# A cubic in depressed form for VectorE's share of the softmax exponentials

## The chip, the cores and the metric

The kernel runs on one core of one Trainium2 chip. The metric is the device time of one execution in microseconds (us), and a kernel's time is the median of its runs. A profile is one execution, taken by the hardware profiler. The engines are written as in the profile: PE is TensorE (matmuls), ACT is ScalarE, DVE is VectorE, POOL is GpSimd, SP is SyncE.

## The reference

Two layers follow one another, each an attention block and a token mixer. Cut to what matters:

```python
def _A_ref(x, wqkv, wo):                    # x: 1 x 2048 x 640, 32 heads of 20
    qkv = ...                               # x @ wqkv, split into q, k, v by heads
    scores = einsum("bhqd,bhkd->bhqk", q, k) * (Dh ** -0.5)
    p = softmax(scores, axis=-1)
    o = einsum("bhqk,bhkd->bhqd", p, v)
    return ... @ wo
def _B_ref(x, w1, b1, w2, b2):              # mixes tokens: 2048 -> 1536 -> 2048
    h = layernorm(x)
    u = gelu(einsum("bsd,sf->bdf", h, w1) + b1)
    return ...                              # einsum("bdf,fs->bds", u, w2) + b2, transposed
x = x + _A_ref(layernorm(x), A_wqkv, A_wo)
x = x + _B_ref(layernorm(x), B_w1, B_b1, B_w2, B_b2)
...                                         # the same two lines once more
```

A layer needs 32 x 2048 x 2048 exponentials of scores. They are by far the largest elementwise work.

## The kernel before

**Units and chunks.** A layer's attention is cut into 512 units: one block of 512 queries, one group of four heads, one tile of 128 keys. Each unit has four chunks, one for a head: 128 keys by 512 queries of scores. `s_matmul` (L703) makes the scores of a chunk in PSUM, already scaled so that the integer part is the power of two wanted times 65536. `emit_PV` (L1334) multiplies the exponentials of a unit with the values (`Vaug`) and adds to `acc`.

**Who takes the exponentials.** `emit_exp` (L773) gives two or three chunks at a time to ScalarE, from a tile `S` to a tile `P`. Some chunks go to VectorE instead. `ve_admit` takes one chunk at a time while the bank `Dt` is free, VectorE's backlog is at most 7 us and at most two pairs are waiting; two chunks make a pair `p`.

**VectorE's exponential.** It builds the bits of a bf16 number as an integer, in these steps of a pair:

- `first` (L563), once for each chunk: adds 127 * 65536 to the score in `Dt`, clips at zero and writes an int32 to the tile `ew`. Its upper 16 bits are the exponent (`whole`), its lower 16 the fraction (`frac`). Both are read with a step of two 16-bit words.
- `shift` (L661): a shifted fraction in f16, to the tile `ey`. Mostly done by GpSimd, chunk by chunk (`ve_shift`), on VectorE only where GpSimd has not done it (`shifted`).
- `squared` (L593): `ey` times itself, 1024 columns, in place.
- `mantissa` (L597): (ey + constant) * frac, one three-operand instruction over 1024 columns, to the tile `et` as an int16. There is one `et` buffer.
- `expo` (L614 and L616): 128 * whole + et, to `Pd`, read as bf16 by the product. GpSimd may already have written 128 * whole for a chunk (`ve_base`, L644). If it did so for both, VectorE adds `et` in one instruction (L614, 1024 columns). If for none, one three-operand instruction does it all (L616, 1024 columns). If for one, each half has its own instruction (L614 and L616, 512 columns).

**What sets the order.** The order on VectorE, ScalarE and GpSimd is written out when the program is built, by a planner that replays the engines with constants for the cost of every step. `Proc` is a chain of steps; `Proc.step` moves the engine's clock to the step's end less 0.083 (`DVE_OVER`) and lets the chain's next step start 0.034 (`DVE_NEXT`) after that end. `pump` picks, of the chains that can start, the one of the lowest rank; evacuations for TensorE have ranks 0 to 2, a pair's chain has 4, and only the oldest pair may go on. The costs of a pair's steps stand in one place:

```python
cost = VE_ADD[min(2, len(ve_based.get(p, [])) + 2 - k)]    # VE_ADD = (1.22, 1.03, 0.69)
steps += [(0.69, squared, 0.0, True), (1.22, mantissa, 0.0, True), (cost, expo, 0.0, True)]
```

The last `True` marks steps beside which GpSimd gets no work. GpSimd's `shift` and base steps are put beside VectorE's other steps of at least 0.45 us, and each waits for the VectorE instruction ahead of that host (`after_vector`).

TensorE's queue follows the same plan; where nothing useful is due it gets products with zeros (`zero_wave`, L762). VectorE takes exponentials in the first layer from early on, in the second one only after the mixer of the layer before has been worked off beside the first units.

Of the kernel before, what the change touches and what calls it, by code (L numbers as in the profile page):

```python
# [15 lines left out]
I16 = mybir.dt.int16  # L16
U16 = mybir.dt.uint16
F16 = mybir.dt.float16
ACT = mybir.ActivationFunctionType
ALU = mybir.AluOpType  # L20
# [43 lines left out]
POOL_BASE_HOST = 0.45  # L64
VEP_BUFS = 4
VE_SPARE = 6
VE_ADD = (1.22, 1.03, 0.69)
POOL_DMA = 0.9

HOLD = 3  # L70
# [1 line left out]
LOG2E = 1.4426950408889634  # L72
LN2 = 0.6931471805599453
FIX = 65536.0
MANT = (0.07706715865, 0.22764486, 0.69511682)
MANT_S = -0.5 * MANT[1] / MANT[0]
MANT_C = MANT[2] / MANT[0] - MANT_S ** 2
MANT_K = (MANT[0] * 128.0 / FIX) ** 0.5


@with_exitstack
def kernel(
# [12 lines left out]
    nc = tc.nc  # L95
# [11 lines left out]
    def after_vector(inst):  # L107
        earlier = next(i for i in reversed(nc.cur_bb.bb.instructions) if i.engine == nc.vector.engine)
        tc.add_manual_dep(inst.ins, earlier.name,
                          mybir.DependencyInfo(mybir.DependencyClass.Sync, mybir.DependencyReason.DATA), reason="port")  # L110
# [113 lines left out]
    def attention(st, x_in_ap, x_mid, uacc_l, feed, feed_stack):  # L224
# [14 lines left out]
        late, ve = {}, {}  # L239
# [284 lines left out]
        def ve_admit(t):  # L524
# [41 lines left out]
            def firsted(end):  # L566
                pieces.append((p, slot, w, end))
                bases.append((p, slot, w, end))
                if slot == 1:
                    ve_enqueue(p, 2, end + DVE_NEXT)  # L570
# [5 lines left out]
        def ve_enqueue(p, k, ready):  # L576
            w = ve_w.pop(p)
            wh = w[:, 0:k, :].rearrange("p a b -> p (a b)").bitcast(I16).rearrange("p (c two) -> p c two", two=2)
            frac = wh[:, :, 0].bitcast(U16)
            whole = wh[:, :, 1]  # L580
            box = {}

            def shifted(end):
                todo = [x for x in range(k) if x not in ve_shifted[p]]
                c0, c1 = 512 * todo[0], 512 * (todo[-1] + 1)
                for x in list(pieces):
                    if x[0] == p:
                        pieces.remove(x)
                shift(nc.vector, ve_y_of(p)[:, c0:c1], frac[:, c0:c1])

            def squared(end):
                y = ve_y_of(p)[:, 0:512 * k]
                nc.vector.tensor_tensor(out=y, in0=y, in1=y, op=ALU.mult)  # L593

            def mantissa(end):
                box["t"] = ve["vet"].tile([128, 1024], I16, name="et")
                nc.vector.scalar_tensor_tensor(out=box["t"][:, 0:512 * k], in0=ve_y.pop(p)[:, 0:512 * k],  # L597
                                               scalar=MANT_C * MANT_K ** 2, in1=frac, op0=ALU.add, op1=ALU.mult)

            def expo(end):  # L600
                Pd = ve_result(p)
                ve_P[p] = Pd
                ve_ready[p] = end + DVE_TO_PE
                ve_procs.popleft()
                for x in [x for x in bases if x[0] == p]:
                    bases.remove(x)
                based = ve_based.pop(p, [])
                parts = [range(k)] if len(based) in (0, k) else [[x] for x in range(k)]
                for part in parts:
                    lo, hi = 512 * part[0], 512 * (part[-1] + 1)  # L610
                    bits = Pd[:, 0:k, :].rearrange("p a b -> p (a b)").bitcast(I16)[:, lo:hi]
                    t = box["t"][:, lo:hi]
                    if part[0] in based:
                        nc.vector.tensor_tensor(out=bits, in0=bits, in1=t, op=ALU.add)  # L614
                    else:
                        nc.vector.scalar_tensor_tensor(out=bits, in0=whole[:, lo:hi], scalar=128.0, in1=t,  # L616
                                                       op0=ALU.mult, op1=ALU.add)
            steps = [(0.15 + 0.27 * (k - len(ve_shifted[p])), shifted, 0.0, True)] if len(ve_shifted[p]) < k else []
            cost = VE_ADD[min(2, len(ve_based.get(p, [])) + 2 - k)]
            steps += [(0.69, squared, 0.0, True), (1.22, mantissa, 0.0, True), (cost, expo, 0.0, True)]  # L620
            proc = Proc(4, steps, ready, allow=lambda me: ve_procs[0] is me and
                        (len(me.steps) > 1 or p in ve_results or p - VEP_BUFS not in ve_users))
            proc.pair, proc.ready = p, max([ready] + ve_shifted_at.get(p, []))
            ve_procs.append(proc)
            dvm["procs"].append(proc)
# [3 lines left out]
        def ve_result(p):  # L629
            if p not in ve_results:  # L630
                ve_results[p] = ve["vep"].tile([128, 2, 512], BF16, name="Pd")
            return ve_results[p]

        def ve_base(at):
            for x in bases:
                p, slot, w, end = x
                if end + POOL_NEXT > at + POOL_LATE or port["t"] > at + POOL_LATE:
                    return
                if p not in ve_results and (p - VEP_BUFS in ve_users or p - 1 not in ve_results and p > 0):
                    return  # L640
                bases.remove(x)
                bits = ve_result(p)[:, slot, :].bitcast(I16)
                whole = w[:, slot, :].bitcast(I16).rearrange("p (c two) -> p c two", two=2)[:, :, 1]
                after_vector(nc.gpsimd.tensor_scalar(out=bits, in0=whole, scalar1=128.0, scalar2=0.0, op0=ALU.mult, op1=ALU.add))  # L644
                port["pool"] = port["t"] = max(at + POOL_NEXT, end + POOL_NEXT, port["t"]) + POOL_EY
                ve_based.setdefault(p, []).append(slot)
                for proc in ve_procs:
                    if proc.pair == p:
                        cost, fn, wait, lock = proc.steps.pop()
                        proc.steps.append((VE_ADD[len(ve_based[p])], fn, wait, lock))  # L650
                return

        ve_y, ve_shifted, ve_shifted_at = {}, {}, {}

        def ve_y_of(p):
            if p not in ve_y:
                ve_y[p] = ve["vey"].tile([128, 1024], F16, name="ey")
            return ve_y[p]

        def shift(engine, out_ap, in_ap):  # L660
            return engine.tensor_scalar(out=out_ap, in0=in_ap, scalar1=MANT_K / FIX, scalar2=-MANT_K * MANT_S,  # L661
                                        op0=ALU.mult, op1=ALU.add)

        def ve_shift(at, self_cost):
            if (not pieces or pieces[0][3] + POOL_NEXT > at + POOL_LATE or port["t"] > at + POOL_LATE or
                    pieces[0][0] - 2 in ve_y):
                if self_cost >= POOL_BASE_HOST:
                    ve_base(at)
                return
            p, slot, w, end = pieces.popleft()  # L670
            half = w[:, slot, :].bitcast(I16).rearrange("p (c two) -> p c two", two=2)[:, :, 0].bitcast(U16)
            inst = shift(nc.gpsimd, ve_y_of(p)[:, 512 * slot:512 * (slot + 1)], half)
            after_vector(inst)
            done = max(at + POOL_NEXT, end + POOL_NEXT, port["t"]) + POOL_EY
            port["pool"] = port["t"] = done
            ve_shifted[p].append(slot)
            ve_shifted_at.setdefault(p, []).append(done + POOL_TO_DVE)
            for proc in ve_procs:
                if proc.pair == p:
                    cost, fn, wait, lock = proc.steps.popleft()  # L680
                    if cost > 0.5:
                        proc.steps.appendleft((cost - 0.27, fn, wait, lock))
                    proc.ready = max(proc.ready, done + POOL_TO_DVE)
# [749 lines left out]
        t = 0  # L1433
# [423 lines left out]
    with ExitStack() as a_stack:  # L1857
        st0 = open_a_scope(0, a_stack)
        open_p_scope(st0, a_stack)
        feed_stack = ExitStack()  # L1860
        feed = TokenFeed(feed_stack)
        attention(st0, A_x[0], xd[0], uacc[0], feed, feed_stack)
    with ExitStack() as a_stack:
        st1 = open_a_scope(1, a_stack)
        open_p_scope(st1, a_stack)
        feed_stack = ExitStack()
        feed = MixFeed(feed_stack, xd[0], xd[1], st0.ua)
        attention(st1, xd[1], xd[0], uacc[1], feed, feed_stack)
# [32 lines left out]
```

## Time and profile before

| | |
|---|---|
| median of 3 runs | 1750.6 us (1750.33 to 1750.99) |
| the profiled execution | 1751.01 us, span 1748.9 us |
| granted TensorE clock | 1.00 |
| busy: PE, ACT, DVE, POOL | 1666.2, 1666.9, 1538.9, 599.6 us |
| L773, exponentials on ACT | 1429 instructions, 1617.1 us |
| L563 to L616, exponentials on DVE | 262 pairs of chunks |
| L762, products with zeros on PE | 324.6 us |

Busy times are those of the profiled execution; the span runs from its first instruction to its last, and the rest of its time lies around that. A row of the profile's groups reads: line, engine, operation, output<-inputs by the program's names, shapes, number, then the busy time in us and the mean of one instruction in ns, then the idle time ahead of them and what ended most of it. VectorE's instructions overlap at their ends, so their durations add up to more than the engine's time.

### The profile page before, as it was taken

The page shows a single profiled execution, that of the slowest core. Times are in us where ns is not written, and L with a number is a line of the kernel's source. Part 1 is how long each engine was busy: PE and PEld are TensorE (multiplying, and loading weights), DVE is VectorE, ACT ScalarE, POOL GpSimd, SP SyncE. Part 2 cuts the span into 40 slices and gives each one's busy share as a digit, 9 for nine tenths or more (in the row PEclk, how much of TensorE's full clock was granted, in tenths as well). Part 3 has the DMA queues.
Part 4 walks back from the last instruction along what each step waited for, and adds up shares of the span by engine and source line. Part 5 has one row for each costly group of instructions (what it writes and reads, how often), then busy time and mean ns, then how long its engine had stood idle before and what let it go on. Part 6 is the DMA issues. An engine that isn't in the chain of part 4 may idle for free.

```text
span 1748.9 us, 43173 instructions
## 1 busy us (share of the span) xinstructions
PE 1666.2 (95%) x17767; PEld 664.3 (38%) x17848; DVE 1538.9 (88%) x2502; ACT 1666.9 (95%) x1498; POOL 599.6 (34%) x948
## 2 busy tenths in 40 slices
PE   8999999999999999999999999999999999999999
PEld 3333333333333343444444433333333333444445
DVE  7789999999999999998544479999999999999973
ACT  9999999999999999999779999999999999999970
POOL 2243443353544343332000023444434443534410
PEclk9999999999999999999999999999999999999999
DMA  4020000000122010133322200001001220211345
GB/s 117 9 23 10 1 2 2 24 24 2 35 66 83 25 42 7 40 90 104 116 78 75 65 11 1 1 2 39 24 2 54 63 85 20 92 29 29 81 121 176
DMA packets 103062, 81.85 MB, mean 47 GB/s; under 512 B 51025, under 2 KB 87505, under 8 KB 102865
## 3 DMA queue, kind: packets, MB, share of 16 engines
q1 hardware_dynamic: 97328, 71.22, 13.8%
q0 software_dynamic: 5536, 7.88, 1.4%
q8 instruction: 139, 2.28, 0.6%
q14 instruction: 59, 0.48, 0.1%
HBM read 55.48 MB, written 23.59 MB: 45 GB/s over the span
## 4 chain that ended last, share of the span: by engine, by line
ACT 51%; PE 25%; issue 22%; DVE 1%; DMA 0%; SPq 0%; another core or an unknown queue 0%; POOL 0%; ACTq 0%; DVEq 0%
ACT P L773 51%; PE S L703 7%; PE acc L1334 4%; PE ya L1784 2%; PE misc L1075 2%; PE acc L762 2%; PE misc L1184 2%; PE um L1771 1%; PE Dt L1184 1%; PE ya L1793 1%; PE yb L1784 1%; PE misc L1124 0%; PE Dt L1703 0%; PE misc L1208 0%; PE misc L1703 0%
## 5 line engine op out<-in xcount | busy, mean ns | idle before, releaser
L773 ACT ACTIVATE P<-S 128x1536 bf16<-128x1536 f32 (+1 forms) x1429 | 1617.1, 1373 | 13.5 <-PE S L703 13.1
L703 PE MATMUL S<-QTq,KT 32*128 32x512 bf16 (+1 forms) x4476 | 578.2, 336 | 65.0 <-ACT P L773 48.3
L661 POOL TENSOR_SCALAR ey<-ew 128x512 f16<-128x512 uint16 x512 | 317.8, 621 | 681.7 <-DVE et L597 295.5
L703 PEld LDWEIGHTS <-KT 32*128 32x128 bf16 x5152 | 232.3, 91 | 524.8 <-issue 497.4
L563 DVE TENSOR_SCALAR ew<-Dt 128x512 int32<-128x512 f32 x524 | 357.0, 681 | 21.2 <-PE Dt L703 14.7
L1334 PE MATMUL acc<-P,Vaug 128*32 128x512 bf16 (+1 forms) x4444 | 362.2, 343 | 0.1
L597 DVE SCALAR_TENSOR_TENSOR et<-ey,ew 128x1024 int16<-128x1024 f16 x262 | 326.0, 1244 | 2.8
L762 PE MATMUL acc<-zr,zw 128*32 128x512 bf16 x4184 | 324.6, 382 | 1.2 <-POOL zr L155 1.2
L644 POOL TENSOR_SCALAR Pd<-ew 128x512 int16<-128x512 int16 x333 | 206.8, 626 | 168.4 <-DVE et L597 44.7
L703 PE MATMUL Dt<-QTq,KT 32*128 32x512 bf16 (+1 forms) x676 | 201.4, 334 | 0.0
L593 DVE TENSOR_TENSOR ey<-ey 128x1024 f16<-128x1024 f16 x262 | 189.5, 723 | 1.4 <-POOL ey L661 0.3
L1334 PEld LDWEIGHTS <-Vaug 128*32 128x32 bf16 x5120 | 102.5, 94 | 169.5 <-issue 157.5
L762 PEld LDWEIGHTS <-zw 128*32 128x32 bf16 x4408 | 111.1, 96 | 96.7 <-issue 50.9
L614 DVE TENSOR_TENSOR Pd<-Pd,et 128x1024 int16<-128x1024 int16 (+1 forms) x197 | 129.8, 659 | 5.5 <-POOL Pd L644 3.3
L616 DVE SCALAR_TENSOR_TENSOR Pd<-ew,et 128x1024 int16<-128x1024 int16 (+1 forms) x126 | 123.5, 980 | 0.6
L903 POOL TENSOR_TENSOR rstd<-veps,mhalf 128x1 f32<-128x1 f32 x60 | 49.8, 830 | 212.9 <-DVE veps L901 194.1
L1334 PE MATMUL acc<-Pd,Vaug 128*32 128x512 bf16 (+1 forms) x676 | 103.0, 337 | 0.3 <-DVE Pd L614 0.2
L1184 PE MATMUL misc<-hh,wq_pad 128*128 128x512 bf16 x255 | 75.8, 383 | 2.8 <-issue 1.6
L1184 PE MATMUL misc<-hh,wk_pad 128*128 128x512 bf16 x240 | 73.3, 383 | 2.6 <-issue 1.9
L1075 PEld LDWEIGHTS <-w1st 128*128 128x128 bf16 x672 | 52.5, 97 | 57.6 <-issue 45.4
L1124 PE MATMUL misc<-wo_pad,attnT 128*128 128x320 bf16 x384 | 72.1, 302 | 0.0
L1075 PE MATMUL misc<-x1last,w1st 128*128 128x320 bf16 x384 | 71.8, 302 | 0.0
(146 smaller groups left out, 1187.5 us busy)
## 6 DMA issues: line engine op xcount, KB each, us to landing
w2s<-in_B_w_dram SPq DMA_DIRECT2D x16, 768.0 KB
uacc<-ustg POOLq DMA_DIRECT2D x24, 320.0 KB, 2.7
x1in<-xd SPq DMA_DIRECT2D x24, 320.0 KB
w1st<-in_B_w_dram SPq DMA_DIRECT2D x24, 256.0 KB
xd<-x2s SPq DMA_DIRECT2D x16, 320.0 KB
xin<-xd SPq DMA_DIRECT2D x16, 320.0 KB
w1st<-in_B_w_dram SPq DMA_DIRECT2D x21, 192.0 KB
xd<-x1s SPq DMA_DIRECT2D x12, 320.0 KB
```

The source lines that it names most:

```text
L563: nc.vector.tensor_scalar(out=w[:, slot, :], in0=Dt[:, :], scalar1=127.0 * FIX, scalar2=0.0, op0=ALU.add, op1=ALU.max)
L593: nc.vector.tensor_tensor(out=y, in0=y, in1=y, op=ALU.mult)
L597: nc.vector.scalar_tensor_tensor(out=box["t"][:, 0:512 * k], in0=ve_y.pop(p)[:, 0:512 * k], scalar=MANT_C * MANT_K ** 2, in1=frac, op0=ALU ...
L614: nc.vector.tensor_tensor(out=bits, in0=bits, in1=t, op=ALU.add)
L644: after_vector(nc.gpsimd.tensor_scalar(out=bits, in0=whole, scalar1=128.0, scalar2=0.0, op0=ALU.mult, op1=ALU.add))
L661: return engine.tensor_scalar(out=out_ap, in0=in_ap, scalar1=MANT_K / FIX, scalar2=-MANT_K * MANT_S, op0=ALU.mult, op1=ALU.add)
L703: pe(nc.tensor.matmul(out_ap[:, c0:c0 + w], lhsT=KT[32 * j:32 * j + 32, g, kt * 128:(kt + 1) * 128], rhs=get_QT(st, qb)[32 * j:32 * j + 32 ...
L762: pe(nc.tensor.matmul(bank[32 * j:32 * j + 32, 0:w], lhsT=zw[:], rhs=zr[:, :, 0:64].to_broadcast([128, w // 64, 64]), start=start, stop=st ...
L773: nc.scalar.activation(out=P[:, 0:ncs, :].rearrange("p a b -> p (a b)"), in_=St[:, 0:ncs, :].rearrange("p a b -> p (a b)"), func=ACT.Exp, ...
L1075: pe(nc.tensor.matmul(t[:, 0:w], lhsT=w1_of[(p, ft)][:, sti, :], rhs=rows_in[sti][:, c0:c1], start=(sti == 0), stop=(sti == n_in - 1)))
L1184: pe(nc.tensor.matmul(t[:, :], lhsT=wpad[:, dt_, g, :], rhs=hT[:, dt_, tb * 512:(tb + 1) * 512], start=(dt_ == 0), stop=(dt_ == NDT - 1)))
L1334: pe(nc.tensor.matmul(acc[32 * j:32 * j + 32, a0:a0 + w], lhsT=Vaug[:, (kt * H + hh_) * VW:(kt * H + hh_) * VW + 32], rhs=P[:, slot, c0:c0 ...
```

## The change

The polynomial for the fraction f, a cubic through 0 at 0 and about 128 at 1, is written without its quadratic term: with y proportional to f + 0.916 it is y * (y * y + A) - 66. The steps become:

- `squared` writes y * y to `et` (now an f16 tile) and leaves y in `ey`.
- `slope`, new: adds the constant A to `et` in place, one input, 1024 columns of f16.
- `mantissa`: `et` times `ey`, two inputs, f16 in, int16 out, in place in `et`.
- `expo`: the -66 goes into the base, 128 * whole - 66. Halves without a base from GpSimd get it from VectorE in one `set_base` instruction; then one addition of 1024 columns follows in all three cases.

The shift has other constants. The planner's costs become 0.69, 0.43, 0.69 and (1.3, 1.03, 0.69).

```diff
-VE_ADD = (1.22, 1.03, 0.69)
+VE_ADD = (1.3, 1.03, 0.69)
+VE_SLOPE = 0.43
...
-MANT = (0.07706715865, 0.22764486, 0.69511682)
-MANT_S = -0.5 * MANT[1] / MANT[0]
-MANT_C = MANT[2] / MANT[0] - MANT_S ** 2
-MANT_K = (MANT[0] * 128.0 / FIX) ** 0.5
+MANT_0 = -66.0
+MANT = (0.08063961, 0.49462884, -0.91643084)
+MANT_K = (128.0 * MANT[0]) ** (1.0 / 3.0)
+MANT_A = 128.0 * MANT[1] / MANT_K
...
             def squared(end):
                 y = ve_y_of(p)[:, 0:512 * k]
-                nc.vector.tensor_tensor(out=y, in0=y, in1=y, op=ALU.mult)
+                box["q"] = ve["vet"].tile([128, 1024], F16, name="et")
+                nc.vector.tensor_tensor(out=box["q"][:, 0:512 * k], in0=y, in1=y, op=ALU.mult)
+
+            def slope(end):
+                q = box["q"][:, 0:512 * k]
+                nc.vector.tensor_scalar(out=q, in0=q, scalar1=MANT_A, scalar2=None, op0=ALU.add)
 
             def mantissa(end):
-                box["t"] = ve["vet"].tile([128, 1024], I16, name="et")
-                nc.vector.scalar_tensor_tensor(out=box["t"][:, 0:512 * k], in0=ve_y.pop(p)[:, 0:512 * k],
-                                               scalar=MANT_C * MANT_K ** 2, in1=frac, op0=ALU.add, op1=ALU.mult)
+                box["t"] = box["q"][:].bitcast(I16)
+                nc.vector.tensor_tensor(out=box["t"][:, 0:512 * k], in0=box["q"][:, 0:512 * k],
+                                        in1=ve_y.pop(p)[:, 0:512 * k], op=ALU.mult)
...
-                parts = [range(k)] if len(based) in (0, k) else [[x] for x in range(k)]
-                for part in parts:
-                    lo, hi = 512 * part[0], 512 * (part[-1] + 1)
-                    bits = Pd[:, 0:k, :].rearrange("p a b -> p (a b)").bitcast(I16)[:, lo:hi]
-                    t = box["t"][:, lo:hi]
-                    if part[0] in based:
-                        nc.vector.tensor_tensor(out=bits, in0=bits, in1=t, op=ALU.add)
-                    else:
-                        nc.vector.scalar_tensor_tensor(out=bits, in0=whole[:, lo:hi], scalar=128.0, in1=t,
-                                                       op0=ALU.mult, op1=ALU.add)
+                bits = Pd[:, 0:k, :].rearrange("p a b -> p (a b)").bitcast(I16)
+                todo = [x for x in range(k) if x not in based]
+                if todo:
+                    lo, hi = 512 * todo[0], 512 * (todo[-1] + 1)
+                    set_base(nc.vector, bits[:, lo:hi], whole[:, lo:hi])
+                nc.vector.tensor_tensor(out=bits, in0=bits, in1=box["t"][:, 0:512 * k], op=ALU.add)
...
-            steps += [(0.69, squared, 0.0, True), (1.22, mantissa, 0.0, True), (cost, expo, 0.0, True)]
+            steps += [(0.69, squared, 0.0, True), (VE_SLOPE, slope, 0.0, True), (0.69, mantissa, 0.0, True), (cost, expo, 0.0, True)]
...
+        def set_base(engine, out_ap, in_ap):
+            return engine.tensor_scalar(out=out_ap, in0=in_ap, scalar1=128.0, scalar2=MANT_0, op0=ALU.mult, op1=ALU.add)
...
-                after_vector(nc.gpsimd.tensor_scalar(out=bits, in0=whole, scalar1=128.0, scalar2=0.0, op0=ALU.mult, op1=ALU.add))
+                after_vector(set_base(nc.gpsimd, bits, whole))
...
-            return engine.tensor_scalar(out=out_ap, in0=in_ap, scalar1=MANT_K / FIX, scalar2=-MANT_K * MANT_S,
+            return engine.tensor_scalar(out=out_ap, in0=in_ap, scalar1=MANT_K / FIX, scalar2=-MANT_K * MANT[2],
                                         op0=ALU.mult, op1=ALU.add)
```

## The prediction

> **What bounds the kernel now.** I read the page's busy sums and slices first, then its costliest groups.
>
> ```profile
> PE 1666.2 (95%) x17767; PEld 664.3 (38%) x17848; DVE 1538.9 (88%) x2502; ACT 1666.9 (95%) x1498; POOL 599.6 (34%) x948
> ...
> DVE  7789999999999999998544479999999999999973
> ACT  9999999999999999999779999999999999999970
> ...
> L773 ACT ACTIVATE P<-S 128x1536 bf16<-128x1536 f32 (+1 forms) x1429 | 1617.1, 1373 | 13.5 <-PE S L703 13.1
> ```
>
> ScalarE (ACT) is full from the first slices to the last but one, and one line fills it, the exponentials of L773. VectorE (DVE) is full in two long stretches with a hole between. Next the busy time in stages of 50 us:
>
> ```profile
> core 0: us, PE busy (x) PEld busy (x) DVE busy (x) ACT busy (x) POOL busy (x), PEclk, DMA share, GB/s
> 400.00:450.00 50.00, 47.51 (x478) 15.31 (x479) 49.23 (x69) 50.00 (x45) 19.45 (x33) 1.00 0.00 1
> 900.00:950.00 50.00, 48.26 (x379) 20.23 (x379) 20.55 (x44) 50.00 (x45) 2.20 (x4) 1.00 0.19 56
> 1100.00:1150.00 50.00, 47.36 (x405) 15.22 (x410) 49.30 (x71) 50.00 (x46) 22.48 (x37) 1.00 0.00 1
> ```
>
> In 150 to 800 and 1050 to 1650 us both engines are full. There are 2 layers x 512 units x 4 heads = 4096 chunks of 512 columns; VectorE takes 524 of them, in 262 pairs, ScalarE the other 3572. So a chunk is worth 1617.1 / 3572 = 0.453 us of ScalarE, and the change pays only through the planner: cheaper pairs, more pairs admitted, fewer chunks for L773. TensorE (PE) is 95% busy, but 324.6 us of that are the filler products of L762 (acc<-zr,zw), so it is no second wall. Last, VectorE's groups with shapes kept apart, then its timeline:
>
> ```profile
> L563 DVE TENSOR_SCALAR ew<-Dt 128x512 int32<-128x512 f32 x524 | 357.0, 681 | 21.2 <-PE Dt L703 14.7 <-PE S L703 1.2
> L597 DVE SCALAR_TENSOR_TENSOR et<-ey,ew 128x1024 int16<-128x1024 f16 x262 | 326.0, 1244 | 2.8
> L593 DVE TENSOR_TENSOR ey<-ey 128x1024 f16<-128x1024 f16 x262 | 189.5, 723 | 1.4 <-POOL ey L661 0.3
> L614 DVE TENSOR_TENSOR Pd<-Pd,et 128x1024 int16<-128x1024 int16 x136 | 102.3, 752 | 3.5 <-POOL Pd L644 2.0
> L616 DVE SCALAR_TENSOR_TENSOR Pd<-ew,et 128x1024 int16<-128x1024 int16 x65 | 82.0, 1261 | 0.6
> L616 DVE SCALAR_TENSOR_TENSOR Pd<-ew,et 128x512 int16<-128x512 int16 x61 | 41.6, 681 | 0.0
> L614 DVE TENSOR_TENSOR Pd<-Pd,et 128x512 int16<-128x512 int16 x61 | 27.5, 450 | 2.0 <-POOL Pd L644 1.3
> L907 DVE TENSOR_SCALAR h_bf<-x0in,mv,rstd 128x640 bf16<-128x640 bf16 x16 | 7.0, 439 | 2.5 <-POOL rstd L903 0.8 <-PE misc L1232 0.8 <-PE Dt L1232 0.7
> L907 DVE TENSOR_SCALAR h_bf<-x2s,mv,rstd 128x640 bf16<-128x640 f32 x11 | 6.7, 609 | 6.7 <-POOL rstd L903 6.6
> L661 DVE TENSOR_SCALAR ey<-ew 128x512 f16<-128x512 uint16 x12 | 5.1, 428 | 0.2
> ```
>
> ```profile
> 1109.41 0.74 DVE L593 TENSOR_TENSOR ey<-ey 128x1024 f16<-128x1024 f16 x1
> 1110.19 1.23 DVE L597 SCALAR_TENSOR_TENSOR et<-ey,ew 128x1024 int16<-128x1024 f16 x1
> 1111.35 0.69 DVE L370 CAST KT<-misc 128x512 bf16<-128x512 f32 x1
> ```
>
> L597 needs L593 and starts 0.034 us after its end; the unrelated L370 starts 0.08 us before L597's end. So an instruction occupies its duration less 0.083 us, and 0.117 more when its neighbour needs it. Walking the timeline, start to next start, a pair costs 2 x 0.617 (L563) + 0.717 (L593) + 1.199 (L597) + 0.897 (the last step over its three cases) = 4.05 us.
>
> **The middle step.** Medians, here and below, are from the answers for single lines and forms; they hold fewer waits for GpSimd than the means. L597 (median 1.225, occupies 1.142) goes; a one-input step and a two-input step of 1024 columns come. The two-input one is L593's form with an integer output: 0.683, occupies 0.600. The one-input dense 16-bit step is not in the trace at this size, so I work out its rate. L616's medians, 1.226 for 1024 columns and 0.681 for 512, give 1.06 ns a column (call it one a cycle) and 0.137 fixed. L661, 0.418 for 512 strided columns, is left with 0.281: two a cycle. The 16-bit L907 row takes 0.170 us less than its f32 twin for the same 640 columns, 0.27 ns a column: a quarter of a cycle, the step from two a cycle to four. At four, 1024 columns stream as long as L661's 512 at two. So 0.418, occupies 0.335. Bounds: 0.361 (L661's shortest) below; 0.683 above, should it run at two a cycle as L593 does. Saving 1.142 - 0.935 = 0.207, less one more dependent link. 82 of 262 squarings now have L597 right behind; with a shorter step I take 4 in 10: 0.4 x 0.117 = 0.047. That leaves 0.160 us x 262 = 42 us.
>
> [...]
>
> **The last step.** Where GpSimd (POOL) made both bases (136 pairs) nothing changes. For none (65): 1.142 now; then a strided step of 0.418 + 0.272 = 0.690 (512 columns more at two a cycle), a link, and 0.683, together 0.690 + 0.034 + 0.683 - 0.083 = 1.324, so +0.18, 12 us. For one (61): 0.598 + 0.367 now, 0.418 + 0.034 + 0.600 then, +0.087, 5 us. GpSimd's own base step (L644, 621 ns) only gets another constant.
>
> **A wait that comes in.** The squaring now writes the single et buffer, which the last step of the pair before still reads. In the trace's records 61 of 524 L563, whose input comes from TensorE alone, also wait on VectorE's own semaphore; so I expect such a wait. It costs 0.117 where the two are neighbours, 89 of 262 times: 10 us; 0 if none is set. Behind it stand the next Dt evacuation and GpSimd's ey job, which is tied to the instruction before its host.
>
> VectorE's real saving: 42 - 12 - 5 - 10 = 15 us. With every doubtful term at its best (a step of 0.361, no more neighbours, no wait) it is 15 + 15 + 12 + 10 = 52; with links always paid, 15 - 18 = -3; with the step at 0.683 too, -72.
>
> **What the planner does with it.** It orders by its own constants, 1.22 against 0.43 + 0.69. Never neighbours, a pair saves 1.22 - (0.43 - 0.083 + 0.69) = 0.183; always, 0.066; at 4 in 10, 0.136 x 262 = 36 us, less 0.08 x 65 for the dearer case: 31 us. With x pairs more the time falls by 2 x 0.453 = 0.906x, and 31 = 3.93x + 0.906x gives x = 6.4, 13 chunks, **-5.8 us** (the two ends: -8.0, and -2.3).
>
> Can VectorE deliver it? It idles 28 us in the two full stretches (14.7 and 13.4 by the stages). It must do 6.4 x 4.0 = 26 us more, less 15, in 5.8 us less: 17 of the 28 are used. Results reach TensorE a median of about 4 us after they are written (pairing last steps with the products in order), a further buffer. So the sum holds, with 11 us, 0.04 us a pair, to spare.
>
> The profiled execution took 1751.0 (span 1748.9 and 2.1 around it), 0.4 over the median of 1750.6. Less 5.8: 1745.2 for it, **1745** for the median.
>
> **Rivals.** *The new link always drains VectorE* (1747 to 1754), though the plan overlaps it: the saving is 24 us for 42, -3 in all, the demand 26 + 3 + 5.8 = 35 of the 28 us of idle time, and 7 us come back: 1750.6 - 5.8 + 7 = 1752. If the planner sees the neighbours itself, it admits less and gains its 2.3: 1748. [...] For it: the 82 squarings that already pay the link. Against: the 180 that do not, with starts 0.07 to 0.08 us before the end of the one in front.
>
> *VectorE is over-committed* (slower): the plan books 31 us and the engine frees 15. Place: Pd for L1334, then L773 starved. Every 0.01 us that a pair costs beyond my sum is 2.7 us; the 0.04 to spare goes first, and at 0.063 the gain is used up. At 0.1 it is 16 - 5.8, about 1761; if the 28 us of idle time, mostly waits for TensorE, cover nothing, the 16 us not freed all show, again 1761; with both, some 1770. For it: the base steps on VectorE are booked 0.10 us too low. Against: in 676 products TensorE now waits 0.2 us for Pd, and 44 waits of L563 for Dt say that VectorE runs ahead of its orders.
>
> *The one-input step does not reach four columns a cycle in f16*: +0.265 x 268 = 71 us, of which 11 are covered; 1745 + 60 = 1805. Against: the bf16 row.
>
> **How the numbers follow.** Forecast (1741 to 1747) 0.46; draining links 0.22; over-commitment 0.28; the slow step 0.04. About 0.2%, 3.5 us, is what a measurement of this kernel can tell from no change. So faster 0.46, same 0.22, slower 0.32. Range 1740 to 1765: below lies only a saving above its bound, above the far end of the over-commitment and the slow step. The forecast's own range is 1741 to 1747.
>
> **What would show it.** Right: some 268 pairs, L773 near 1611 us, the new one-input row at 0.42, the two-input row at 0.68 to 0.72, VectorE idle falling from 28 to some 11 us in the full stretches, ScalarE still at 50 of 50. Wrong: idle time of TensorE ended by Pd, gaps ahead of L773, a one-input row near 0.68, or no more than 264 pairs.

## The result and the profile after

The changed kernel takes 1757.38 us (median of 6 runs, 1756.12 to 1759.11) against 1750.89 for the kernel before: ratio 1.0038, interval 1.0028 to 1.0048. It is slower by 6.5 us. The profiled execution took 1756.98 us, its span is 1755.1.

The ScalarE group that answers to L773 (now L778):

```profile
L778 ACT ACTIVATE P<-S 128x1536 bf16<-128x1536 f32 (+1 forms) x1427 | 1615.2, 1371 | 20.5 <-PE S L708 14.1
```

ScalarE has a little less to do than before (1615.2 for 1617.1 us), as a kernel with more pairs on VectorE should, and still ends later. So it idled. The stages show where; this is the one that differs most, before and after:

```profile
100.00:150.00 50.00, 46.62 (x387) 17.12 (x389) 44.28 (x73) 50.00 (x45) 22.76 (x29) 1.00 0.23 27
...
100.00:150.00 50.00, 43.50 (x353) 14.92 (x352) 42.02 (x65) 43.29 (x39) 25.07 (x33) 0.93 0.20 23
```

ScalarE (fourth busy figure) works 43.29 of 50 us where it worked 50.00, and the granted clock of TensorE is 0.93 where it was 1.00. This one stage loses 6.7 us. VectorE's groups for a pair, behind its first steps and shifts and without the 49 base steps of a single half (L637, 23.4 us):

```profile
L595 DVE TENSOR_TENSOR et<-ey 128x1024 f16<-128x1024 f16 x265 | 190.4, 718 | 9.1 <-DVE Pd L619 0.5
L619 DVE TENSOR_TENSOR Pd<-Pd,et 128x1024 int16<-128x1024 int16 x265 | 189.0, 713 | 15.1 <-POOL Pd L637 2.5
L603 DVE TENSOR_TENSOR et<-et,ey 128x1024 int16<-128x1024 f16 x265 | 188.1, 710 | 4.7
L599 DVE TENSOR_SCALAR et<-et 128x1024 f16<-128x1024 f16 x265 | 122.6, 463 | 2.7
L637 DVE TENSOR_SCALAR Pd<-ew 128x1024 int16<-128x1024 int16 x74 | 52.6, 711 | 0.0
```

The one-input step (L599) has a median of 0.427 us, the product (L603) one of 0.693, close to the 0.418 and 0.683 of the forecast. There are 265 pairs, three more than before. The longest L599 took 4727 ns. The timeline there, VectorE, GpSimd and TensorE in turn:

```profile
118.72 4.73 DVE L599 TENSOR_SCALAR et<-et 128x1024 f16<-128x1024 f16 x1
123.37 0.67 DVE L564 TENSOR_SCALAR ew<-Dt 128x512 int32<-128x512 f32 x1
...
126.25 0.69 DVE L619 TENSOR_TENSOR Pd<-Pd,et 128x1024 int16<-128x1024 int16 x1 [1.60 <-POOL Pd L637]
...
118.81 4.37 POOL L1519 MEMSET wo_pad<- 128x5120 bf16 x1
...
125.61 0.61 POOL L637 TENSOR_SCALAR Pd<-ew 128x512 int16<-128x512 int16 x1
...
124.10 0.37 PE L708 MATMUL Dt<-QTq,KT 32*128 32x512 bf16 x1 [2.95 <-DVE ew L564]
...
127.40 1.49 PE L1213 MATMUL misc<-x1last,hh 128*128 128x320 bf16 x5 [2.06 <-DVE Vaug L371]
```

The lines hold two delays. GpSimd's zeroing of `wo_pad`, which happens once, is in both.

First, the one-input step is issued beside the zeroing and ends only after it: 4.73 us instead of 0.43. The evacuation of `Dt` (L564) stands behind it on VectorE, the next product into `Dt` behind that on TensorE, and so the scores for ScalarE. This is TensorE's idle stretch of 2.95 us.

Second, the pair's last step (L619) needs a base from GpSimd (L637). GpSimd makes it only at 125.61 us, behind the zeroing and two DMA issues of 1.24 and 1.18 us (L184 and L185, for the biases), none of which the planner books. VectorE waits 1.60 us for it, the evacuation of `misc` (`Vaug`, L371) stands behind that, and TensorE idles for another 2.06 us. The order on VectorE is fixed when the program is built, so this last step, and all behind it, could not have started before 126.2 us even if the one-input step had not been held. The chain that the profile follows back from 128 us agrees: it runs through the zeroing, the two DMA issues, the base and the last step, and not through L599.

In the second stretch, from 125.7 us, the granted clock falls to 0.50 for 6.83 us; it shows as 1.00 again from 132.6 us. The kernel before has the same zeroing at the same place:

```profile
119.38 1.26 DVE L597 SCALAR_TENSOR_TENSOR et<-ey,ew 128x1024 int16<-128x1024 f16 x1
120.67 0.43 DVE L614 TENSOR_TENSOR Pd<-Pd,et 128x512 int16<-128x512 int16 x1
121.01 0.68 DVE L616 SCALAR_TENSOR_TENSOR Pd<-ew,et 128x512 int16<-128x512 int16 x1
...
119.62 4.37 POOL L1514 MEMSET wo_pad<- 128x5120 bf16 x1
```

There a three-operand step, a two-input step and another three-operand step run beside it at their usual length (1.26, 0.43 and 0.68 us; the means of these forms are 1.244, 0.450 and 0.681), and the pair waits for no base: VectorE makes the missing one itself, in L616.

So at this place the one-input step was held (4.73 us for 0.43) and the two other forms were not. The expectations below call this hold "the port", a name for it and no more: no run shows what in the chip causes it. The experiments ask what of the time it explains, and whether it goes by the form of VectorE's step or by what GpSimd's instruction does.

### The profile page after: what moved, and what is told of

It is laid out like the page before. It is cut to its first block, busy times and chain, and to the rows that moved or that the text cites. A ratio compares the mean times of both kernels' runs of the same rounds, so it can differ in the third digit from the quotient of the medians.

```text
span 1755.1 us, 43730 instructions
## 1 busy us (share of the span) xinstructions
PE 1677.1 (96%) x17884; PEld 663.6 (38%) x17884; DVE 1537.0 (88%) x2840; ACT 1664.9 (95%) x1496; POOL 591.8 (34%) x958
## 4 chain that ended last, share of the span: by engine, by line
ACT 41%; PE 22%; issue 19%; DVE 16%; POOL 1%; DMA 1%; SPq 0%; DVEq 0%; ACTq 0%; POOLq 0%
ACT P L778 41%; PE S L708 6%; DVE ew L564 4%; PE acc L1339 3%; PE ya L1789 2%; DVE Pd L619 2%; DVE et L595 2%; DVE et L603 2%; PE acc L767 2%; PE misc L1189 2%; DVE Pd L637 1%; PE misc L1080 1%; DVE et L599 1%; PE um L1776 1%; PE ya L1798 1%
## 5 line engine op out<-in xcount | busy, mean ns | idle before, releaser
L778 ACT ACTIVATE P<-S 128x1536 bf16<-128x1536 f32 (+1 forms) x1427 | 1615.2, 1371 | 20.5 <-PE S L708 14.1
L708 PEld LDWEIGHTS <-KT 32*128 32x128 bf16 x5136 | 227.6, 91 | 526.6 <-issue 498.6
L564 DVE TENSOR_SCALAR ew<-Dt 128x512 int32<-128x512 f32 x530 | 361.3, 682 | 13.7 <-PE Dt L708 9.3
L1339 PE MATMUL acc<-P,Vaug 128*32 128x512 bf16 (+1 forms) x4434 | 362.2, 343 | 0.4 <-DVE T L815 0.3
L767 PE MATMUL acc<-zr,zw 128*32 128x512 bf16 x4276 | 330.0, 384 | 1.2 <-POOL zr L156 1.2
L637 POOL TENSOR_SCALAR Pd<-ew 128x512 int16<-128x512 int16 x333 | 204.0, 617 | 158.3 <-DVE et L595 42.8
L619 DVE TENSOR_TENSOR Pd<-Pd,et 128x1024 int16<-128x1024 int16 x265 | 189.0, 713 | 15.1 <-POOL Pd L637 2.5
L595 DVE TENSOR_TENSOR et<-ey 128x1024 f16<-128x1024 f16 x265 | 190.4, 718 | 9.1 <-DVE Pd L619 0.5
L603 DVE TENSOR_TENSOR et<-et,ey 128x1024 int16<-128x1024 f16 x265 | 188.1, 710 | 4.7
L1339 PEld LDWEIGHTS <-Vaug 128*32 128x32 bf16 x5120 | 101.9, 94 | 178.3 <-issue 165.0
L599 DVE TENSOR_SCALAR et<-et 128x1024 f16<-128x1024 f16 x265 | 122.6, 463 | 2.7
L908 POOL TENSOR_TENSOR rstd<-veps,mhalf 128x1 f32<-128x1 f32 x60 | 41.8, 697 | 216.6 <-DVE veps L906 193.5
L1339 PE MATMUL acc<-Pd,Vaug 128*32 128x512 bf16 (+1 forms) x686 | 104.4, 336 | 0.3 <-DVE Pd L619 0.2
L1189 PE MATMUL misc<-hh,wq_pad 128*128 128x512 bf16 x290 | 85.0, 383 | 0.8 <-DVE QTq L373 0.7
L1189 PE MATMUL misc<-hh,wk_pad 128*128 128x512 bf16 x270 | 79.0, 383 | 0.0
L637 DVE TENSOR_SCALAR Pd<-ew 128x1024 int16<-128x1024 int16 (+1 forms) x123 | 76.0, 618 | 0.0
```

Of the source, the lines that this page charges most:

```text
L564: nc.vector.tensor_scalar(out=w[:, slot, :], in0=Dt[:, :], scalar1=127.0 * FIX, scalar2=0.0, op0=ALU.add, op1=ALU.max)
L595: nc.vector.tensor_tensor(out=box["q"][:, 0:512 * k], in0=y, in1=y, op=ALU.mult)
L603: nc.vector.tensor_tensor(out=box["t"][:, 0:512 * k], in0=box["q"][:, 0:512 * k], in1=ve_y.pop(p)[:, 0:512 * k], op=ALU.mult)
L619: nc.vector.tensor_tensor(out=bits, in0=bits, in1=box["t"][:, 0:512 * k], op=ALU.add)
L637: return engine.tensor_scalar(out=out_ap, in0=in_ap, scalar1=128.0, scalar2=MANT_0, op0=ALU.mult, op1=ALU.add)
L708: pe(nc.tensor.matmul(out_ap[:, c0:c0 + w], lhsT=KT[32 * j:32 * j + 32, g, kt * 128:(kt + 1) * 128], rhs=get_QT(st, qb)[32 * j:32 * j + 32 ...
```

## The experiments

Of a pair's chain, "link" is a step that starts right behind the one it needs, 0.034 us after its end; an unrelated one starts 0.08 us before that end. Where sums of ScalarE are given, they come from walking its instructions from the first exponential to the last: the time of that phase is ScalarE's busy time and its idle time, 1640.2 + 23.7 us before, 1638.3 + 31.9 after.

**1. The changed kernel without the collision** (timed against before, as are 2 to 7 and 9).

```diff
-            nc.gpsimd.memset(wo_pad[:], 0.0)        # TokenFeed.after_end
...
             cx.open_psum()                          # TokenFeed.begin
+            nc.gpsimd.memset(wo_pad[:], 0.0)
```

> The changed kernel, with GpSimd's zeroing of wo_pad moved from 119 us to the start, ahead of VectorE's first exponential. Theory (the port): the new one-input step was held by that one zeroing, TensorE ran dry and its clock halved, and this is the whole loss; so the 4.7 us step is gone, the longest one-input step is under 1.3 us, the clock is 1.00 and the time is 1757.4 - 6.7, about 1749 to 1751. Rival (the chain): VectorE is late everywhere through its links and the et wait, and the zeroing was only where it showed; so the time stays at 1755 or more and ScalarE's gaps turn up elsewhere.

1751.59 us, ratio 1.0004 (0.9995 to 1.0013), clock 1.00, no step of over 1.3 us. ScalarE: 1638.2 + 25.5. The zeroing at that place was the whole loss. The run takes both delays away at once, the held step and the base behind the zeroing, so it doesn't say how much of the loss was the held step's alone. Nothing is won either; ScalarE's 2.0 us less work meets 1.8 us more idle time. Of these, 0.7 are still in the stage from 100 to 150 us (ScalarE busy 49.26 of 50), where the base now stands behind the two DMA issues alone and the last step waits 1.59 us for it.

**2. The same move in the kernel before.**

> The kernel before, with the same move of the zeroing. Theory (the port): its three-operand step ran beside the zeroing in 1.26 us, so nothing was lost there and nothing is won: 1750 to 1751.5. Rival (the zeroing costs any kernel time through the port): 1748 or less.

1751.63 us, ratio 1.0002 (0.9993 to 1.0011). The zeroing had cost the kernel before nothing. Both kernels now stand level, so without the collision the change is worth nothing measurable.

**3. The zeroing in its place, in eight pieces.**

```diff
-            nc.gpsimd.memset(wo_pad[:], 0.0)
+            for g in range(NG):
+                nc.gpsimd.memset(wo_pad[:, g, :], 0.0)
```

> The changed kernel, the zeroing left in its place but cut into eight pieces of 640 columns. Theory (the port, held for one instruction at a time): VectorE gets in between two pieces, so no VectorE instruction there takes over 1.3 us, the clock stays at 1.00 and the time is 1749 to 1752. Rival (the port is given to GpSimd for as long as it has work queued): a step of over 4 us remains and 1757. Rival (the chain): 1755 or more.

1758.06 us, ratio 1.0039 (1.0026 to 1.0052). The first rival's numbers came, a step of over 4 us and some 1757. The timeline's VectorE and GpSimd rows:

```profile
119.11 5.00 DVE L599 TENSOR_SCALAR et<-et 128x1024 f16<-128x1024 f16 x1
...
119.20 4.64 POOL L1520 MEMSET wo_pad<- 128x640 bf16 x8
```

VectorE's step ended 0.27 us after the last of the eight pieces that GpSimd had queued back to back, not between two of them. The last step waits for its base here too, 1.61 us.

**4. The split undone: one three-operand instruction in depressed form.**

```diff
-            steps += [(0.69, squared, 0.0, True), (VE_SLOPE, slope, 0.0, True), (0.69, mantissa, 0.0, True), (cost, expo, 0.0, True)]
+            steps += [(0.69, squared, 0.0, True), (1.22, mantissa, 0.0, True), (cost, expo, 0.0, True)]
...                                                  # in mantissa:
-                nc.vector.tensor_tensor(out=box["t"][:, 0:512 * k], in0=box["q"][:, 0:512 * k],
-                                        in1=ve_y.pop(p)[:, 0:512 * k], op=ALU.mult)
+                nc.vector.scalar_tensor_tensor(out=box["t"][:, 0:512 * k], in0=box["q"][:, 0:512 * k], scalar=MANT_A,
+                                               in1=ve_y.pop(p)[:, 0:512 * k], op0=ALU.add, op1=ALU.mult)
```

> The changed kernel with its one-input and two-input step put back into one three-operand instruction, (y*y + A) * y, at the old planned cost of 1.22; the dearer last step and the wait for et stay. Theory (the port): a two-operand form is not held by a zeroing that reads nothing, so no long step, clock 1.00; what is left is the dearer last step and the wait, some 0 to 4 us over before: 1750.5 to 1754.5. Rival (the chain: base steps and the et wait made VectorE late): at least half of the loss stays, 1754 to 1757.

1759.85 us, ratio 1.0052 (1.0040 to 1.0065): outside both. The timeline says why the theory's number failed though the three-operand form was not held:

```profile
118.67 1.25 DVE L603 SCALAR_TENSOR_TENSOR et<-et,ey 128x1024 int16<-128x1024 f16 x1
119.84 3.59 DVE L637 TENSOR_SCALAR Pd<-ew 128x512 int16<-128x512 int16 x1
...
118.79 4.36 POOL L1519 MEMSET wo_pad<- 128x5120 bf16 x1
```

The three-operand step runs beside the zeroing in 1.25 us; the base step behind it, which the change also made a one-input instruction, is held for 3.59. I had overlooked it. The rest fits a dearer last step without a cheaper middle: 261 pairs, ScalarE 1643.5 + 29.3, both more than before. Of the idle time only 2.7 us lie in the stage from 100 to 150 us. In that stage no base of GpSimd is waited for, so here the held step alone kept VectorE back.

**8. The kernel before, with a zeroing that reads** (one profiled run).

```diff
-            nc.gpsimd.memset(wo_pad[:], 0.0)
+            nc.gpsimd.tensor_scalar(out=wo_pad[:].rearrange("p g d -> p (g d)"),
+                                    in0=wq_pad[:].rearrange("p a g c -> p (a g c)"),
+                                    scalar1=0.0, scalar2=0.0, op0=ALU.mult, op1=ALU.add)
```

> The kernel before, with wo_pad zeroed in the old place by an instruction of GpSimd that reads SBUF (another tile times zero) instead of one that only writes. [...] Rival (two-input instructions are never held by GpSimd for long): the step stays under 1.7 us and the time at 1751 to 1752.

1754.94 us, above the rival's 1751 to 1752, and with a step far over its 1.7 us. The three-operand step started ahead of the GpSimd instruction and took its usual time; the two-input one behind it is held:

```profile
118.77 1.25 DVE L597 SCALAR_TENSOR_TENSOR et<-ey,ew 128x1024 int16<-128x1024 f16 x1
120.06 4.56 DVE L614 TENSOR_TENSOR Pd<-Pd,et 128x512 int16<-128x512 int16 x1
...
119.03 5.31 POOL L1514 TENSOR_SCALAR wo_pad<-wq_pad 128x5120 bf16<-128x5120 bf16 x1
```

The same two-input form took 0.43 us beside the zeroing that only writes. So both the form and the GpSimd instruction mattered in these runs: one-input steps were held beside a GpSimd instruction that only writes (4.73 us in the changed kernel, 3.59 in run 4), a two-input step beside the reading one and not beside the writing one (4.56 against 0.43). In small, longer steps go with GpSimd's jobs all along: in run 1, each of the 130 steps behind the shift that took over 0.1 us more than the median of its form overlaps one of GpSimd's shift or base jobs, which read. No base of GpSimd is waited for in run 8, so there the held step alone cost some 4 us (1754.94 against 1750.72, one run).

Then the second question: why is the change worth nothing even without the collision?

**5. No wait for `et`**, on top of 1: the product goes to `ey`, which is given back after the last step.

```diff
-                box["t"] = box["q"][:].bitcast(I16)
+                box["t"] = ve_y_of(p)[:].bitcast(I16)
...                                                  # ve_y.pop(p) moves from the product to expo
```

> The changed kernel with the zeroing at the start (as in the first run), and the product written to ey in place of et, so that et is free after the product and the next pair's squaring has nothing to wait for behind the last step. 265 pairs as there. Theory (the wait makes VectorE late): the 96 starts that came 0.104 us after the last step's end come 0.08 before it, 18 us of VectorE come back, and of the 1.8 us by which ScalarE idled longer than before the larger part goes: 1749.5 to 1751. Rival (VectorE had time for the wait): 1751.6, unchanged.

1749.25 us, ratio 0.9991 (0.9982 to 1.0000); ScalarE 1637.1 + 24.5. The theory's number, though the interval touches no change. Of the 2.3 us to run 1, 1.0 are idle time of ScalarE, as the theory has it; another 1.1 are less work for ScalarE at the same 265 pairs, which it doesn't cover. The wait that goes is this one, in the changed kernel's timeline:

```profile
413.09 0.69 DVE L619 TENSOR_TENSOR Pd<-Pd,et 128x1024 int16<-128x1024 int16 x1
413.89 0.69 DVE L595 TENSOR_TENSOR et<-ey 128x1024 f16<-128x1024 f16 x1
```

The squaring starts 0.104 us after the last step of the pair before. So do 55 of the 96 such neighbours in run 1; the other 41 start 0.034 us after it, so the wait was worth 15 us and not the 18 expected. Now 105 neighbours start 0.082 before that end.

**6. Two pairs' chains alternate**, on top of 1, with two buffers for `et` and three in place of four for `Pd`.

```diff
-VEP_BUFS = 4
+VEP_BUFS = 3
...
-            for name, bufs in (("vew", 3), ("vet", 1), ("vey", 2), ("vep", VEP_BUFS)):
+            for name, bufs in (("vew", 3), ("vet", 2), ("vey", 2), ("vep", VEP_BUFS)):
...
-            proc = Proc(4, steps, ready, allow=lambda me: ve_procs[0] is me and
-                        (len(me.steps) > 1 or p in ve_results or p - VEP_BUFS not in ve_users))
+            proc = Proc(4, steps, ready, allow=lambda me: (ve_procs[0] is me and
+                        (len(me.steps) > 1 or p in ve_results or p - VEP_BUFS not in ve_users)) or
+                        (len(ve_procs) > 1 and ve_procs[1] is me and len(me.steps) > 1))
```

> The changed kernel with the zeroing at the start, two et buffers (and three Pd buffers for four, to make room), and the planner allowed to run the next pair's steps, its last one excepted, between the oldest pair's. Theory (the saving went into links): with other work between dependent steps the planner admits some 272 pairs for 265, 14 chunks or 6.3 us less for ScalarE, and the time is 1744 to 1747. Rival (VectorE is full on the chip, whatever the plan says): the added pairs come late, TensorE waits for Pd and the time is 1750 or more.

1742.54 us, ratio 0.9955 (0.9941 to 0.9968): faster than both kernels, and the best of this study. ScalarE 1631.2 + 23.9; 272 pairs. Its ScalarE group and timeline:

```profile
L779 ACT ACTIVATE P<-S 128x1536 bf16<-128x1536 f32 (+1 forms) x1422 | 1608.1, 1378 | 12.5 <-PE S L709 11.9 <-PE acc L1340 0.2
...
453.16 0.42 DVE L599 TENSOR_SCALAR et<-et 128x1024 f16<-128x1024 f16 x1
453.49 0.68 DVE L595 TENSOR_TENSOR et<-ey 128x1024 f16<-128x1024 f16 x1
454.09 0.68 DVE L603 TENSOR_TENSOR et<-et,ey 128x1024 int16<-128x1024 f16 x1
```

The next pair's squaring fills the gap between one pair's one-input step and its product. Only 11 of 272 products still follow their one-input step directly; in the changed kernel 138 of 265 do. Walking VectorE's timeline start to next start, a pair costs 4.05 us before, 4.07 in run 1, 4.03 in run 5 and 3.76 here. Not in these sums are the shifts that GpSimd leaves to VectorE, 109 here for 8 in run 1; with them it is 3.90 for 4.08.

**7. The same freedom for the kernel before**, with its zeroing at the start.

> The kernel before with the zeroing at the start and the same freedom and buffers as the run beside it. It has one dependent link less in a pair to lose, so by the theory of the links it gains less: some 264 pairs for 262, 1749 to 1751. Rival (the freedom helps any chain alike): it gains as much as the changed kernel does, 1744 to 1747.

1751.32 us, ratio 1.0005 (0.9996 to 1.0013), 264 pairs: just above the theory's range. A pair costs 3.93 us, but 73 shifts fall to VectorE, and with these it is 4.04 for the 4.07 of the kernel before: hardly a saving, and the kernel doesn't gain. The freedom pays with the change, not without it.

**9. The buffers of run 6 without the alternation.**

> The changed kernel with the zeroing at the start, two et buffers and three Pd buffers, as in the run with alternating pairs, but with only the oldest pair's steps allowed, as in the change. 264 pairs. Theory (the links): the buffers only remove the wait for et, so the time is that of the run that wrote the product to ey, 1749 to 1751, and the 138 products that follow their one-input step directly are still there. Rival (the buffers, not the alternation, made the faster run): 1746 or less.

1750.52 us, ratio 0.9999 (0.9990 to 1.0008), 264 pairs, 132 direct links from the one-input step to the product. It is the alternation that makes run 6 fast, not the buffers.

## Why the prediction was wrong, step by step

Two things failed. The sum put the contact with GpSimd at nothing, and this is the loss. And the saving of 15 us on VectorE, from which the gain was to come, was not there. The second comes first, term by term.

**The middle step** was forecast to save 0.160 us a pair, by 0.335 + 0.600 for 1.142. The rates were right (medians of 0.427 and 0.693 for 0.418 and 0.683). In run 1 squaring, one-input step and product occupy 0.684 + 0.442 + 0.683 = 1.81 us, against 0.717 + 1.199 = 1.92 before: 0.107 saved, 28 us for 42. The links were under-counted, 4 in 10 assumed and 138 of 265 counted for the product alone; by the prediction's 0.117 that is 4 us. The other 10 are in the durations: the means of the two new steps are 0.448 and 0.711, 0.058 over the forecast's figures, where the old step's mean was 0.019 over its median. Half of that are the medians. The other half are steps that take over 0.1 us more beside a GpSimd job: 55 of them in run 1, together 10 us, for 26 and 5 us before.

**The last step and the wait** were forecast at 12 + 5 + 10 us. Last and base steps cost 0.718 + 123 x 0.682 / 265 = 1.035 us a pair in run 1, against 0.897: 0.138 or 37 us instead of 27, the wait included. The wait I expected is there, in 96 neighbours where 89 were counted, but 55 of them are worth 0.187 us (from 0.083 before the end to 0.104 after), not 0.117: 15 us, not 10. The squaring now waits on VectorE and on GpSimd. The sequencer takes a separate wait instruction for it 136 times at L595, 10 times at L593 before; all 55 neighbours have one, and none of the other 41. (Of the 61 waits at L563 from which I expected this, the trace has 45 as instructions of their own.)

So **VectorE's real saving**, forecast at 15 us, is none: 4.05 us a pair before, 4.07 in run 1.

**The planner's 6.4 pairs** were 3, and ScalarE's work fell by 1.9 us in the trace, not 5.8. The failing term is probably again the share of links: the planner also starts a dependent step late, and in a longer chain of which only the oldest pair's may go on, it more often finds nothing else to put there. Run 6 speaks for it by giving it something: 272 pairs and, in L773's place, 1608.1 us for 1617.1.

**The cover** of 11 us of idle time was half right. In run 1 no lateness of VectorE starved ScalarE for long, but ScalarE idled 1.8 us more than before: 1.0 went with the wait (run 5), 0.7 are the base behind the DMA issues.

**What sent the time the other way** is none of these. I costed GpSimd's part by the pair's own jobs ("only gets another constant") and took as upper end for the one-input step its slower rate, 0.683. That bound was wrong: beside the zeroing the step took 4.73 us where the old forms had kept their 1.26, 0.43 and 0.68, and the longest GpSimd instruction in the trace, 4.37 us, was the row to bound it by. The base step was not safe either: GpSimd makes it when its queue comes to it, and behind the zeroing and the DMA issues that was 6.7 us after its job before. With the idle TensorE and its clock behind them, the two are the 6.7 us of the stage at 100 to 150 us. How they share it stays open: no run has the new chain with one of them alone. Run 4 (held step alone, another chain) lacks 2.7 us of ScalarE in that stage, run 8 (held step alone, old chain) 4.3. The time, 1757.4, lies on the slower side, which the prediction gave to the over-commitment rival (1761 to 1770 by its figures), but that mechanism was not the cause: TensorE waited for Pd (L1339) 0.2 us in all, and the starvation came at one place. That the time still lies in the wide range of 1740 to 1765 is luck. The rival of the draining links comes nearer in its time to what was left over after the collision: it says 1748 to 1752, and run 1 is 1751.6. No run shows that VectorE drains at a link; what the changed kernel shows is that 138 of its 265 products start 0.033 to 0.035 us after the end of their one-input step.

## What to carry to other kernels

When an instruction is replaced by faster ones, ask whether the new forms have been seen at their usual length beside the other engines' instructions, as the old one was, and set them against the longest of those, even one that runs once: here GpSimd's zeroing of 4.37 us, beside which the new step took 4.73 us for 0.43. Ask also what stands in that engine's queue behind it: a short job that a planner puts there comes late by all of it (a base of 0.61 us came 6.7 us after GpSimd's job before), and a stall can have two causes that end together. Splitting a fused step needs something independent to fill each new gap; this change was worth nothing alone and 8 us with two chains interleaved. Here TensorE's idle stretches of 2.95 and 2.06 us also came with 6.83 us at a granted clock of 0.50, from 0.4 us into the second; what that adds was not measured by itself.

## What the runs showed of the hardware

Not expected: eight zeroing instructions queued back to back on GpSimd held a one-input VectorE step for 5.00 us, one big one for 4.73. A squaring starts 0.034 us after the last step it waits for (41 of 41 neighbours in run 1), and 0.104 us after it where the sequencer has a separate wait instruction for it (55 of 55). The end of the span left aside, half-clock stretches lasted 3.41 us (run 4) or 6.83 (changed kernel, runs 3 and 8) after TensorE had been idle for 1.5 to 3.2 us at a stretch. Run 3 has one more, of 3.41 us at 893 us, where no idle stretch is over 0.9 us; its cause is open.
